# Splitting the first and the last loads of a gated attention and feed-forward kernel

## The chip, the cores and the metric

The kernel runs on one core of one Trainium2 chip. The metric is the device time of one execution in microseconds. Times are medians over repeated executions. The profile is of one further execution. Its span runs from the first to the last recorded instruction, and the execution's own time is a little longer than the span.

## The reference, cut to what matters

Four sequences each decode one token `x` of 512 numbers. One branch is attention with 32 heads over a cache of 4096 keys and values of 128 numbers each, the other a gated feed-forward net. A sigmoid gate mixes the two. All data is float32.

```python
q = (x @ wq).reshape(B, Sq, H, Dh).transpose(0, 2, 1, 3)
scores = einsum("bhqd,bhkd->bhqk", q, k_cache) * (Dh ** -0.5)
o = einsum("bhqk,bhkd->bhqd", softmax(scores), v_cache)
a = o.transpose(0, 2, 1, 3).reshape(B, Sq, H * Dh) @ wo
b = (gelu(x @ w_gate) * (x @ w_up)) @ w_down
g = sigmoid((x * gate_w).sum(-1, keepdims=True))
return g * a + (1 - g) * b
```

`wq` is 512 x 4096, `wo` is 4096 x 512, `w_gate` and `w_up` are 512 x 1792, `w_down` is 1792 x 512. The two caches hold 268 MB each.

## The kernel before, in words

**Tiles.** The caches are cut into 32 steps: four heads of one sequence per step. A step's keys are a tile of 128 partitions by 64 KB (each partition holds 128 whole keys of one head, contiguous in memory), and its values another of the same shape. There are two tiles for keys, `K[0]` and `K[1]`, and one for values, `V`. The weights `wq` have the same shape (128 partitions, four rows of the matrix in each) and are put into `V` before the first values need it.

**Queues.** Every load and store is issued by SyncE, through the helper `load` (L125), whose `dma_start` is L127. The trace therefore puts all DMA issues on L127. SyncE issues in program order and waits between issues until the tile that is to be overwritten is free. Each named load has a semaphore of its own, which counts to 16 when the load has landed.

**The start.** SyncE issues `wq` into `V` (L136), `x` into four partitions (L138), `gate_w` into the same four partitions of another tile (L140), and the first two key tiles. TensorE turns `x` (L163), the gate is worked out from `x` and `gate_w` (L170 to L182, with a matmul at L176), and after that TensorE waits for `have_xT` and `got_q` (L188) and multiplies `x` by `wq` (L193). ScalarE and TensorE turn the result into `QT` (L199 to L211), and the first query is spread over the partitions as `QB[0]` (L218, L221).

**The steps.** `keys(i)` (L266 on) waits for a key tile, multiplies it by the query on VectorE (L269), sums each key's products (L271), and finds the maximum. ScalarE makes the weights (L289). TensorE, in a loop of its own, multiplies them with the values (L231) once these have landed. SyncE issues keys `i + 2` when the sums of step `i` are done (L310) and values `i + 1` when the matmuls of step `i` are done (L313).

**The end.** Into the two key tiles go the weights of the feed-forward net, and then `wo`. `wo` has 32 rows in each partition. Eighteen of them are loaded behind `w_down` in `K[1]`, in two loads of 10 and 8 rows (L326). The last fourteen are loaded into `K[0]` in the sizes of `PIECES` (L55), one load per size (L361 to L364), issued as soon as the feed-forward net no longer needs this tile. A row is 2 KB in each partition, 256 KB in all.

TensorE takes the pieces in order (L418 to L430): it waits for piece `k`, and then runs four matmuls for each of its rows, one per quarter of the 512 outputs (in the trace each is two). VectorE copies the sum out (L432), SyncE stores it (L433).

```python
    PIECES = (4, 4, 3, 2, 1)
    got_q = load(V, wq.rearrange("(p c) n -> p (c n)", c=KC), name="got_q")
    PE.wait(have_xT, got_q)
        PE.wait(got_w[k])
```

Of the kernel before, what the change touches and what calls it, by code (L numbers as in the profile page):

```python
# [34 lines left out]
def tile_gated_mix(ctx: ExitStack, tc: tile.TileContext, x, kc, vc, wq, wo, w_gate, w_up, w_down, gate_w, out):  # L35
    nc = tc.nc
    P = 128
# [3 lines left out]
    KC = DM // P  # L41
# [10 lines left out]
    W1 = (TW - DR * DM) // DM  # L52
    WR = TW // DM
    W0 = 10
    PIECES = (4, 4, 3, 2, 1)  # L55
    BASE = 24576
    scale = 1.0 / math.sqrt(D)
    c_gelu = math.sqrt(2.0 / math.pi)
# [22 lines left out]
    V = kv.tile([P, TW], F32, name="v")  # L81
# [25 lines left out]
    def semaphore(name):  # L107
        counters.append(ctx.enter_context(nc.semaphore(name)))
        return counters[-1]
# [3 lines left out]
    PE = Line(nc.tensor, semaphore("pe"))  # L113
# [11 lines left out]
    def load(dst, src, sem=None, name=None):  # L125
        sem = sem or semaphore(name)
        nc.sync.dma_start(dst, src).then_inc(sem, 16)  # L127
        return sem, 16
# [4 lines left out]
    def load_v(i):  # L133
        load(V, heads(vc, i), sem_v)

    got_q = load(V, wq.rearrange("(p c) n -> p (c n)", c=KC), name="got_q")  # L136
    x_sb = o[:B]
    got_x = load(x_sb, x.rearrange("b s d -> (b s) d"), name="got_x")  # L138
    gw = gs[:B]
# [4 lines left out]
    p0 = PL.do(nc.gpsimd.memset(ident, 0.0))  # L144
# [21 lines left out]
    for c in range(KC):  # L166
        have_xT = DV.do(nc.vector.tensor_copy(xT[:, c], xT_ps[:, c, :, None].to_broadcast([P, B, 8])))  # L167
# [17 lines left out]
    HB = HG // 2  # L185
    PO = [po, bank[6]]
    w = V.rearrange("p (c n) -> p c n", c=KC)
    PE.wait(have_xT, got_q)  # L188
    for c in range(KC):
        for s in range(2):  # L190
            for j in range(4):
# [125 lines left out]
    f, down = K[0], K[1]  # L317
# [42 lines left out]
    r0 = 0  # L360
    for n in PIECES:  # L361
        got_w.append(load(f[:, r0 * DM:(r0 + n) * DM], wo_rows[:, (W1 + r0) * DM:(W1 + r0 + n) * DM],
                          name=f"got_w{r0}"))
# [53 lines left out]
    i = 0  # L417
    for k, n in enumerate(PIECES):  # L418
        if k == 1:
# [40 lines left out]
```

## Time and profile before

| | us |
|---|---|
| median of 3 runs | 1312.04 |
| lowest and highest run | 1311.94, 1312.5 |
| the profiled execution's own time | 1312.45 |
| its span | 1310.7 |
| VectorE busy | 1142.5 |
| TensorE busy with matmuls | 390.0 |
| ScalarE busy | 108.7 |

The page's lines in the prediction read as follows. The row `DMA` gives, in 40 equal slices of the span, the busy share of the 16 DMA engines in tenths. The row `q1` is the queue that SyncE fills: packets, MB, and the share of the 16 engines' span that its packets took. The row of percentages by engine is the chain of work that ended last. A row that begins with `L269` is a group of instructions: line, engine, operation, tile written and read, shapes, count, busy time and mean in ns of one, then the idle time of the engine ahead of them and what ended it. Rows such as `k<-in_A_k_cache SPq` are DMA issues: count, KB each where it is given, and the median time in us from issue to landing.

Rows that begin with a time are from the timeline: start, duration, engine, line, operation, tiles, shape, count, and in brackets the idle time ahead and its releaser. Rows that begin with two times joined by a colon are stretches: length, then busy time and count for TensorE, its weight loads, VectorE, ScalarE and GpSimd, then TensorE's granted clock, the DMA share and GB/s. Where such a row was asked for one line alone, it has TensorE's two columns only. A packet counts with its whole size and duration in the stretch in which it starts.

### The profile page before, as it was taken

To read this page: it belongs to the slowest core of one execution; us is meant where nothing else is said; L and a number is where in the kernel's file an instruction comes from. 1 tells how busy PE (TensorE), PEld (TensorE's weight loads), DVE (VectorE), ACT (ScalarE), POOL (GpSimd) and SP (SyncE) were. 2 spreads that over 40 slices of the span, in tenths; PEclk is the share of its full clock that TensorE was granted. 3 is DMA by queue.
4 is the path that set the end of the run, shared out by engine and by line. 5 is a ranking of instruction groups with operands and counts; after the bars stand their busy time and mean duration, and the time that the engine had idled before them with its cause. 6 is when DMAs were issued, how large, how long until landed. Compare 5 with 4: busy or idle time off the path is not lost.

```text
span 1310.7 us, 6525 instructions
## 1 busy us (share of the span) xinstructions
PE 390.0 (30%) x2766; PEld 136.1 (10%) x2766; DVE 1142.5 (87%) x263; ACT 108.7 (8%) x360; POOL 0.7 (0%) x6
## 2 busy tenths in 40 slices
PE   2132123333213333312333321233231133332147
PEld 0010001111001111000111100011010011100012
DVE  1799999999989899998989989998998999899850
ACT  0000111000000000000000000000000000000010
POOL 0000000000000000000000000000000000000000
PEclk9665566666556666656666655666655666665578
DMA  9999999999999999999999999999999999999998
GB/s 417 416 447 428 436 443 422 444 420 448 426 438 438 426 444 420 448 422 442 436 428 444 420 444 424 440 438 428 446 420 444 422 442 436 428 448 418 434 430 342
DMA packets 10846, 564.80 MB, mean 431 GB/s; under 512 B 1212, under 2 KB 1228, under 8 KB 1620
## 3 DMA queue, kind: packets, MB, share of 16 engines
q1 hardware_dynamic: 10836, 564.69, 99.5%
q8 instruction: 4, 0.07, 0.0%
q14 instruction: 6, 0.05, 0.0%
HBM read 564.67 MB, written 0.01 MB: 431 GB/s over the span
## 4 chain that ended last, share of the span: by engine, by line
DMA 51%; DVE 48%; PE 1%; issue 0%; SPq 0%; ACT 0%
DMA k<-in_A_k_cache 45%; DVE k L269 24%; DVE SC L271 24%; DMA k<-in_B_w_up 3%; DMA k<-in_A_wo 3%; PE bank L338 0%; PE bank L428 0%; SPq L127 0%; DVE m L273 0%; DVE k L354 0%; DVE mt L274 0%; DVE k L351 0%; DVE k L352 0%; DVE nm L275 0%; ACT k L349 0%
## 5 line engine op out<-in xcount | busy, mean ns | idle before, releaser
L269 DVE TENSOR_TENSOR k<-k,QB 128x16384 f32<-128x16384 f32 x32 | 551.2, 17225 | 82.6 <-DMA k<-in_A_k_cache 82.6
L271 DVE TENSOR_REDUCE SC<-k 128x128 f32<-128x16384 f32 x32 | 551.0, 17220 | 1.1
L231 PE MATMUL bank<-v,PM 128*16 128x512 f32 x2048 | 294.7, 740 | 569.8 <-PEq L258 555.7
L231 PEld LDWEIGHTS bank<-v,PM 128*16 128x16 f32 x2048 | 69.4, 113 | 768.5 <-issue 754.3
L224 PE MATMUL bank<-RS,ones 128*128 128x4 f32 x64 | 17.7, 347 | 288.0 <-PEq L256 288.0
L308 ACT ACTIVATE o<-bank 128x512 f32<-128x512 f32 x31 | 18.5, 597 | 869.2 <-PE bank L231 869.2
L289 ACT ACTIVATE PM<-SC,nm 32x128 f32<-32x128 f32 x128 | 66.0, 516 | 200.9 <-DVE nm L275 199.4
L224 PEld LDWEIGHTS bank<-RS,ones 128*128 128x128 f32 x64 | 15.8, 306 | 294.3 <-issue 294.3
L237 PE MATMUL bank<-pick,o 128*128 128x4 f32 x256 | 32.9, 252 | 25.1 <-PEq L260 25.1
L237 PEld LDWEIGHTS bank<-pick,o 128*128 128x128 f32 x256 | 31.0, 191 | 53.6 <-issue 52.7
L280 DVE RECIPROCAL ri<-bank 128x4 f32<-128x4 f32 x32 | 5.5, 173 | 22.5 <-PE bank L237 22.5
L289 ACT ACTIVATION_READ_ACCUMULATOR PM<-SC,nm 32x1 f32 x128 | 25.1, 196 | 0.0
L167 DVE COPY xT<-bank 128x32 f32<-128x32 f32 x4 | 0.5, 182 | 21.5 <-PE bank L163 21.5
L218 PE MATMUL bank<-ident,QX 128*128 128x128 f32 x64 | 15.0, 316 | 1.5 <-ACT QX L215 1.5
L221 ACT ACTIVATE QB<-bank 128x128 f32<-128x128 f32 x32 | 8.9, 278 | 47.3 <-PE bank L218 47.3
L432 DVE COPY res<-bank 128x128 f32<-128x128 f32 x1 | 0.3, 292 | 12.5 <-PE bank L428 12.5
L273 DVE TENSOR_REDUCE m<-SC 128x1 f32<-128x128 f32 x32 | 9.2, 286 | 1.1
L215 ACT ACTIVATE QX<-QT 128x128 f32<-128x128 f32 x32 | 9.9, 308 | 2.4 <-DVE QT L209 1.6
L209 DVE COPY QT<-bank 128x16 f32<-128x16 f32 x8 | 0.9, 180 | 10.5 <-PE bank L205 10.5
L218 PEld LDWEIGHTS bank<-ident,QX 128*128 128x128 f32 x64 | 9.7, 192 | 1.9 <-ACT QX L215 1.1
L193 PE MATMUL bank<-v,xT 128*32 128x512 f32 x64 | 9.5, 760 | 0.0
L338 PE MATMUL bank<-k,xT 128*32 128x448 f32 x64 | 8.1, 659 | 2.6 <-DMA k<-in_B_w_up 2.6
(57 smaller groups left out, 63.5 us busy)
## 6 DMA issues: line engine op xcount, KB each, us to landing
k<-in_B_w_gate SPq DMA_DIRECT2D x1, 3584.0 KB, 31.9
k<-in_B_w_up SPq DMA_DIRECT2D x1, 3584.0 KB, 40.0
k<-in_B_w_down SPq DMA_DIRECT2D x1, 3584.0 KB, 29.5
k<-in_A_wo SPq DMA_DIRECT2D x1, 2560.0 KB, 35.2
k<-in_A_wo SPq DMA_DIRECT2D x1, 2048.0 KB, 39.6
k<-in_A_wo SPq DMA_DIRECT2D x2, 1024.0 KB, 33.5
k<-in_A_wo SPq DMA_DIRECT2D x1, 768.0 KB, 35.9
k<-in_A_k_cache SPq DMA_DIRECT2D x32, 42.7
```

Of the source, the lines that this page charges most:

```text
L193: t = nc.tensor.matmul(PO[s][32 * j:32 * j + 32], xT[:, c, :], w[:, c, n0:n0 + HB * D], start=c == 0, stop=c == KC - 1)
L215: return nc.scalar.activation(QX, QT[:, b, HT * g:HT * g + HT, None].to_broadcast([P, HT, PH]), AF.Copy)
L218: return nc.tensor.matmul(qp[:, :D], QX.rearrange("p h k -> p (h k)"), ident, start=True, stop=True)
L221: return AC.do(nc.scalar.activation(QB[i % 2], qp[:, :D], AF.Copy, scale=scale))
L224: return nc.tensor.matmul(tot, ones, RS, start=True, stop=True)
L231: t = nc.tensor.matmul(po[32 * c:32 * c + M], p[:, j * M:(j + 1) * M], V[:, j * RJ * D:(j + 1) * RJ * D], start=j < 4, stop=j >= n - 4)
L237: t = nc.tensor.matmul(quo, o[:, j * D:(j + 1) * D], pick[:, j, :], start=j == 0, stop=j == RJ - 1)
L269: DV.wait(DV.do(nc.vector.tensor_tensor(k, k, QB[i % 2][:, None, :].to_broadcast([P, R, D]), op=OP.mult)))
L271: summed[i] = DV.do(nc.vector.tensor_reduce(sc, k, axis=AX.X, op=OP.add))
L273: DV.wait(DV.do(nc.vector.tensor_reduce(m1, sc, axis=AX.X, op=OP.max)))
L289: t = nc.scalar.activation(PM[s, :, h], SC[i % 2][s, :], AF.Exp, bias=NM[i % 2][s, :], scale=1.0, accum_out=RS[s, h:h + 1])
L308: nc.scalar.activation(o, po, AF.Copy).then_inc(token_a, 1)
```

## The change

The first load, `wq` into `V`, becomes two: partitions 0 to 15, and then partitions 16 to 127. TensorE waits for both before its first matmul with `wq`. The last fourteen rows of `wo` come in six loads instead of five: the piece of two rows becomes two pieces of one row. What is computed, and in which order, stays the same.

```diff
-    PIECES = (4, 4, 3, 2, 1)
+    PIECES = (4, 4, 3, 1, 1, 1)
...
-    got_q = load(V, wq.rearrange("(p c) n -> p (c n)", c=KC), name="got_q")
+    wq_rows = wq.rearrange("(p c) n -> p (c n)", c=KC)
+    got_q = [load(V[p0:p1], wq_rows[p0:p1], name=f"got_q{p0}") for p0, p1 in ((0, 16), (16, P))]
...
-    PE.wait(have_xT, got_q)
+    PE.wait(have_xT, *got_q)
```

## The prediction

> **What bounds the kernel now.** I read the page's summary first, then the chain of work that ended last, then the queue's own waits, and last the two ends of the span, since the change touches only the first load and the last ones.
>
> ```profile
> span 1310.7 us, 6525 instructions
> DMA  9999999999999999999999999999999999999998
> q1 hardware_dynamic: 10836, 564.69, 99.5%
> DMA 51%; DVE 48%; PE 1%; issue 0%; SPq 0%; ACT 0%
> L269 DVE TENSOR_TENSOR k<-k,QB 128x16384 f32<-128x16384 f32 x32 | 551.2, 17225 | 82.6 <-DMA k<-in_A_k_cache 82.6
> k<-in_A_k_cache SPq DMA_DIRECT2D x32, 42.7
> v<-in_A_v_cache SPq DMA_DIRECT2D x32, 29.3
> v<-in_A_wq SPq DMA_DIRECT2D x1, 22.2
> ```
>
> The loads bound it. One queue carries 564.69 MB and holds the 16 DMA engines busy for 99.5% of the span: 564.69 MB / (16 x 0.995 x 1310.7 us) = 27.1 GB/s for each engine. The chain names VectorE for 48%, but VectorE idles 82.6 us in 32 rounds (2.6 us in each) until a key tile lands. A tile is 128 rows of 65,536 B, eight rows per engine. One row takes 65,536 / 27.1 = 2.42 us, a tile 19.35 us. The keys are issued 42.7 us ahead of their landing and the values 29.3 us, so when a load is issued there are some 23 or 10 us of older work in front of it. Nothing in the middle can make up for a delay of the DMA engines: **time lost in the first load is lost at the end**, and VectorE, 2.6 us ahead in each round, merely waits later.
>
> The two ends:
>
> ```profile
> 0.96 0.39 SPq L127 DMA_DIRECT2D v<-in_A_wq  x1
> 1.41 0.37 SPq L127 DMA_DIRECT2D o<-in_A_x  x1
> 2.12 0.91 SPq L127 DMA_DIRECT2D k<-in_A_k_cache  x2
> 23.42 0.61 PE L163 MATMUL bank<-ident,o 4*128 4x4 f32 x4 [23.42 <-DMA o<-in_A_x]
> 26.60 9.51 PE L193 MATMUL bank<-v,xT 128*32 128x512 f32 x64
> 40.90 0.28 ACT L221 ACTIVATE QB<-bank 128x128 f32<-128x128 f32 x1 [0.62 <-PE bank L218]
> 42.58 17.22 DVE L269 TENSOR_TENSOR k<-k,QB 128x16384 f32<-128x16384 f32 x1 [3.70 <-DMA k<-in_A_k_cache]
> ...
> 1304.57 2.76 PE L428 MATMUL bank<-k,o 128*32 128x128 f32 x48 [0.71 <-DMA k<-in_A_wo]
> 1305.82 1.05 PEld L428 LDWEIGHTS bank<-k,o 128*32 128x32 f32 x24 [0.29 <-DMA k<-in_A_wo]
> 1307.39 0.29 DVE res L432
> ```
>
> The weights of the queries land at 0.96 + 22.2 = 23.16 us, x a little later, and the first keys at 42.55. At the end the last 48 matmuls run almost without a break to 1307.37, then the copy and the store.
>
> **Part 1: the first load as 16 and 112 rows.** The bytes are the same. SP issues one load more (0.39 us by the row at 0.96), which moves x, gate_w and both first key loads by that much. They wait in the queue until 23 us anyway (the keys are issued at 2.12 and used at 42.58), so this costs nothing; without that cover it is 0.4 us. TensorE has one wait more ahead of L193, behind which its whole sequence is queued, but L193 starts at 26.60, 3.4 us after the weights have landed, because the gate's matmul ahead of it waits for x. Cost nothing, and 3.4 us of cover if the second part lands later than the first.
>
> What counts is how fast 16 neighbouring rows can be written. No load of before has that shape, so bounds first. Every large load covers 128 partitions, eight per engine. If each engine keeps its pace, its single row takes 2.42 us: **no loss**. If only the write paths of 16 partitions' share (2 of 16) carry it, 1 MiB takes as long as a whole tile, 19.35 us: a loss of 16.9 us. The nearest row is the load of x: four rows to partitions 0 to 3, 8 KB, right behind the weights. TensorE has it at 23.42, 0.26 us after the weights; about 0.04 us of that is the step from landing to start that the chain shows as issue:
>
> ```profile
> 1304.52 0.04 issue
> ```
>
> At 27.1 GB/s 8,192 B take 0.30 us on one path and 0.08 us on four. The 0.22 us left are nearer to one path for four neighbouring partitions. It is thin, since the row doesn't tell which engines carried x, but it is the only row of this kind. Four partitions to a path put 16 rows on 4 paths, four engines on each: 4 x 2.42 = 9.7 us, **a loss of 7.25 us**, and the engines cannot go on to their next row before.
>
> [...]
>
> Then the 112 rows, seven to an engine if they are shared out evenly and in order. Engine boundaries at sevens no longer fall on groups of four partitions, so engines meet on a path while other paths are idle. Bounds: nothing, if they meet nowhere, and 7 x 2.42 = 16.9 us, if the worst-placed engine shares its path in every row. The slowest engine counts, as the next tile is used when all of it has landed. Of its seven rows I take three as shared with one other engine, each at half pace: 3 x 2.42 = **7.25 us**, a choice a little under the middle.
>
> [...]
>
> A gain belongs to the same part: a shorter first load might start the engines sooner. The stretches of the start:
>
> ```profile
> 1.00:2.00 1.00, 0.00 (x0) 0.00 (x0) 0.90 (x5) 1.00 (x1) 0.45 (x2) 1.00 0.20 66
> 2.00:2.40 0.40, 0.00 (x0) 0.00 (x0) 0.40 (x3) 0.19 (x1) 0.00 (x0) 1.00 5.63 1802
> 2.40:2.90 0.50, 0.00 (x0) 0.00 (x0) 0.12 (x2) 0.00 (x0) 0.00 (x0) 1.00 0.73 262
> 2.90:3.40 0.50, 0.00 (x0) 0.00 (x0) 0.00 (x0) 0.00 (x0) 0.00 (x0) 1.00 0.32 131
> 3.40:5.00 1.60, 0.00 (x0) 0.00 (x0) 0.00 (x0) 0.00 (x0) 0.00 (x0) 1.00 0.09 41
> ```
>
> The last two columns book a packet where it starts: most engines begin between 2.0 and 2.4 us, the last after 3.4. Between nothing and 1.5 us (all engines as early as the first) can be gained. I take 0: the row at 0.96 ends its issue at 1.35, no sooner than x's with its four rows, so a small issue is no quicker.
>
> **Part 2: the last rows as 1, 1, 1 instead of 2, 1.**
>
> ```profile
> 1269.53 0.81 SPq L127 DMA_DIRECT2D k<-in_A_wo  x2
> k<-in_A_wo SPq DMA_DIRECT2D x1, 768.0 KB, 35.9
> k<-in_A_wo SPq DMA_DIRECT2D x1, 512.0 KB, 36.2
> k<-in_A_wo SPq DMA_DIRECT2D x1, 256.0 KB, 36.5
> ```
>
> The two-row piece lands at 1269.53 + 36.2 = 1305.7 to 1305.8, the last row some 0.6 us later, at 1306.4. The sequencer stood 0.29 us (PEld at 1305.82) until the two rows were there. With single rows the first lands 0.6 us sooner, that wait goes, and what is late next is the last row itself: landing 1306.4, a start 0.04 later, and 8 matmuls. 24 matmuls a microsecond is the pace there:
>
> ```profile
> 1306.00:1307.00 1.00, 1.00 (x24) 0.80 (x19) 0.50 0.06 18
> L428 PE MATMUL bank<-k,o x112: 268/273/422, 1300.4 to 1306.9; 128*32 128x128 f32 x112
> ```
>
> So 8 take 0.33 us, the last of them up to 0.42 by itself (the second row's longest): 1307.2 instead of 1307.37. Gain 0.1 to 0.2, at most 0.29; I take **0.1**. One more load is issued 0.43 us behind its neighbour, 36 us before it lands: nothing. Its overhead in the engines is unknown, between 0 and the 0.4 us that two issues lie apart; the pieces of 3, 2 and 1 rows land in proportion to their rows, so I take 0.
>
> **The sum.** The profiled execution took 1312.45 us (span 1310.7, 1.75 around it); 1312.45 + 7.25 + 7.25 - 0.1 = 1326.85. The median of the runs is 0.41 lower, so the forecast is **1326.4 us**. One discount stays open: the engines do not end together.
>
> ```profile
> 1304.00:1305.00 1.00, 0.43 (x12) 0.44 (x16) 0.86 0.35 141
> 1305.00:1306.00 1.00, 1.00 (x24) 0.71 (x20) 0.50 0.20 76
> ```
>
> From 1304 on 0.35, then 0.20 of them are busy, so a few end up to 2 us after the rest. If those that lose most at the start are not these, up to 2 us of the loss vanish.
>
> **The rivals.**
>
> *Only the first load is slow.* The 112 rows flow as before. For it: seven rows in a row leave each engine time to shift past its neighbour. Against it: while engines queue for a path, another path idles. 1312.04 + 7.25 - 0.1 = 1319.2, between 1316.5 and 1322.5.
>
> *The engines keep their pace, so it is not slower.* Place: the write of the first 16 rows. It decides if a write path serves each engine, not a group of partitions; then only part 2 and the start count: 1312.04 - 0.1 = 1311.9, between 1310.5 (1.5 us gained at the start) and 1313. For it: the 27.1 GB/s per engine is the same in all loads, whichever partitions an engine writes. Against it: x.
>
> *The 112 rows meet all the time.* If engine e takes every sixteenth row, all 16 engines write 16 neighbouring partitions in each step, each at a quarter of its pace: another 7 x 7.25 = 50.8 us, 1370 us. Against it: the profile shows no load shared out like that.
>
> *The change doesn't do what it says*: the early start of the first load buys nothing since L193 waits for both parts and, before that, for x. That is so in each case above and is in the sum.
>
> **How the numbers follow.** Forecast (1322.5 to 1330): 0.42. Only the first load: 0.24. Pace kept: 0.22. Above 1330: 0.11. Gain over 0.2% by a start that brings more than the 1.5 us: 0.01. The range leaves out the last two and the fringe of others: 1311.0 to 1330.0; the forecast's own is 1322.5 to 1330. About 0.2% (2.6 us) is what a measurement of this kernel can tell from no change. Faster 0.01, same 0.22, slower 0.77.
>
> **What would show it.** Right: the weights land some 14 us later than 23.16 from the first issue, the stretch from 3 to 12 us moves about a quarter of 431 GB/s, the first key product starts near 57 instead of 42.58, every later round is shifted by the same amount, and VectorE's idle time per round stays 2.6 us. If the stretch from 3 to 12 us moves 430 GB/s, the step on the narrow load is wrong. If the key product starts near 50, the step on the 112 rows is. At the end the 0.29 us wait ahead of the last 24 weight loads should be gone. The forecast falls if x was late for a reason of its own, since that row alone chose the value between the bounds.

## The result and the profile after

The changed kernel takes 1333.55 us (median of 6 runs, 1331.57 to 1333.75), the kernel before 1312.03 (6 runs). The ratio is 1.0162, with a 95% interval of 1.0151 to 1.0173: **21.5 us slower**. The forecast was 1326.4 with a range up to 1330.0. The direction was right, and so was the first of the two terms. The second one, for the 112 rows, was half of what it is, because its picture of how engines slow each other was wrong, and the range was too narrow.

The page of the changed kernel first. Lines below L136 of the kernel before have moved down by one.

```profile
span 1331.7 us, 6528 instructions
GB/s 217 378 419 420 441 435 428 439 431 441 429 433 431 439 439 427 437 429 441 431 431 439 431 439 433 431 431 437 439 429 437 429 437 437 429 439 427 429 434 340
q1 hardware_dynamic: 10996, 564.69, 99.5%
L270 DVE TENSOR_TENSOR k<-k,QB 128x16384 f32<-128x16384 f32 x32 | 551.2, 17225 | 84.6 <-DMA k<-in_A_k_cache 84.6
k<-in_A_k_cache SPq DMA_DIRECT2D x32, 42.7
v<-in_A_v_cache SPq DMA_DIRECT2D x32, 29.3
```

The queue moves the same 564.69 MB and is again busy for 99.5% of the span. That share counts the time that packets take, and rows of 64 KB that took 2.4 to 3.6 us in the first load of before now take up to 9.4, so it does not show the loss. The GB/s by slice do: 217 in the first of 40 slices and 378 in the second, where it was 417 and 416, then the old level. The keys and values still land 42.7 and 29.3 us after their issue, as before.

The timeline of the start of the changed kernel:

```profile
0.96 0.87 SPq L127 DMA_DIRECT2D v<-in_A_wq  x2
42.53 0.61 PE L164 MATMUL bank<-ident,o 4*128 4x4 f32 x4 [42.53 <-DMA o<-in_A_x]
45.71 9.82 PE L194 MATMUL bank<-v,xT 128*32 128x512 f32 x64
60.31 0.28 ACT L222 ACTIVATE QB<-bank 128x128 f32<-128x128 f32 x1 [0.62 <-PE bank L219]
63.64 17.22 DVE L270 TENSOR_TENSOR k<-k,QB 128x16384 f32<-128x16384 f32 x1 [5.34 <-DMA k<-in_A_k_cache]
```

The first key product starts at 63.64 instead of 42.58, 21.06 us later, and TensorE's turn of `x` at 42.53 instead of 23.42. Nothing of the 21 us is made up or added in the middle: VectorE's idle time in the 31 rounds after the first is (84.6 - 5.34) / 31 = 2.56 us each, and before it was (82.6 - 3.70) / 31 = 2.55. So the whole loss arises in the first 63 us.

Stretches of the start, of the changed kernel and then of the kernel before; the last two columns are the DMA share and GB/s:

```profile
2.00:12.00 10.00, 0.00 (x0) 0.00 (x0) 0.52 (x3) 0.19 (x1) 0.00 (x0) 1.00 1.33 203
12.00:22.00 10.00, 0.00 (x0) 0.00 (x0) 0.00 (x0) 0.00 (x0) 0.00 (x0) 1.00 0.80 210
22.00:32.00 10.00, 0.00 (x0) 0.00 (x0) 0.00 (x0) 0.00 (x0) 0.00 (x0) 1.00 1.05 262
32.00:42.00 10.00, 0.00 (x0) 0.00 (x0) 0.00 (x0) 0.00 (x0) 0.00 (x0) 1.00 0.97 251
```

```profile
2.00:12.00 10.00, 0.00 (x0) 0.00 (x0) 0.52 (x3) 0.19 (x1) 0.00 (x0) 1.00 1.02 413
12.00:22.00 10.00, 0.00 (x0) 0.00 (x0) 0.00 (x0) 0.00 (x0) 0.00 (x0) 1.00 0.97 419
22.00:32.00 10.00, 6.52 (x34) 2.35 (x38) 2.41 (x10) 0.17 (x1) 0.00 (x0) 1.00 1.08 467
32.00:42.00 10.00, 6.15 (x52) 2.41 (x44) 0.86 (x8) 2.34 (x7) 0.00 (x0) 0.99 1.07 465
```

Both parts of the new first load are slow, and the second one for longer: from 12 to 42 us, while the 112 rows move, the rate is 210 to 262 GB/s where it was 419 to 467. In the trace's packets (64 KB each, one per row) the 16 rows take 7.8 to 9.4 us each instead of 2.4 to 3.6 for the first rows of before. The 112 rows take 4.6 us each in the median. Of an engine's seven rows, the first two take 4.7 to 5.7 us, the third mostly 3.1, the fourth mostly 3.7, and the last three 4.2 to 4.8. **About half pace in five of the seven rows, on every engine,** is what the forecast did not have: it gave three rows of seven to it, and only on the engines that are placed worst.

### The profile page after: what moved, and what is told of

It is laid out like the page before. It is cut to its first block, busy times and chain, and to the rows that moved or that the text cites. A ratio compares the mean times of both kernels' runs of the same rounds, so it can differ in the third digit from the quotient of the medians.

```text
span 1331.7 us, 6528 instructions
## 1 busy us (share of the span) xinstructions
PE 386.2 (29%) x2766; PEld 134.8 (10%) x2766; DVE 1142.4 (86%) x263; ACT 108.7 (8%) x360; POOL 0.7 (0%) x6
## 3 DMA queue, kind: packets, MB, share of 16 engines
q1 hardware_dynamic: 10996, 564.69, 99.5%
## 4 chain that ended last, share of the span: by engine, by line
DMA 50%; DVE 47%; PE 1%; another core or an unknown queue 0%; issue 0%; SPq 0%; ACT 0%; DVEq 0%
DMA k<-in_A_k_cache 41%; DVE k L270 23%; DVE SC L272 23%; DMA o<-in_A_x 3%; DMA k<-in_B_w_up 3%; DMA k<-in_A_wo 3%; PE bank L194 1%; PE bank L339 0%; SPq L127 0%; DVE m L274 0%; ACT v L200 0%; DVE k L355 0%; DVE mt L275 0%; DVE QT L210 0%
## 5 line engine op out<-in xcount | busy, mean ns | idle before, releaser
L270 DVE TENSOR_TENSOR k<-k,QB 128x16384 f32<-128x16384 f32 x32 | 551.2, 17225 | 84.6 <-DMA k<-in_A_k_cache 84.6
L272 DVE TENSOR_REDUCE SC<-k 128x128 f32<-128x16384 f32 x32 | 551.0, 17220 | 1.1
L232 PE MATMUL bank<-v,PM 128*16 128x512 f32 x2048 | 291.7, 734 | 569.8 <-PEq L259 555.4
L281 DVE RECIPROCAL ri<-bank 128x4 f32<-128x4 f32 x32 | 5.5, 172 | 21.8 <-PE bank L238 21.8
```

Source lines behind the costliest of these rows:

```text
L232: t = nc.tensor.matmul(po[32 * c:32 * c + M], p[:, j * M:(j + 1) * M], V[:, j * RJ * D:(j + 1) * RJ * D], start=j < 4, stop=j >= n - 4)
L270: DV.wait(DV.do(nc.vector.tensor_tensor(k, k, QB[i % 2][:, None, :].to_broadcast([P, R, D]), op=OP.mult)))
L272: summed[i] = DV.do(nc.vector.tensor_reduce(sc, k, axis=AX.X, op=OP.add))
```

## The experiments

The experiments are compared with runs of the kernel before on the same chip (1311.99 to 1312.01 us). Four others are ladders, kernels with a series of extra loads ahead of everything; each of these ran once and is read from its trace alone.

### One part at a time

The change without the pieces of `wo`, and the pieces alone:

```diff
+    got_q = [load(V[p0:p1], wq_rows[p0:p1], name=f"got_q{p0}") for p0, p1 in ((0, 16), (16, P))]
```

> Only the first load is split into 16 and 112 rows; the pieces of wo stay 4, 4, 3, 2, 1. Theory (write paths): all of the loss comes from the first load, so 1333.5 us, within 0.5 of the change. Rival (the smaller last pieces, or one more load near the end, cost something): clearly below that, 1333.5 less what they cost. Each would put the landing of the second part at the same time as in the change, 41 to 44 us.

```diff
-    PIECES = (4, 4, 3, 2, 1)
+    PIECES = (4, 4, 3, 1, 1, 1)
```

> Only the last rows of wo come as 4, 4, 3, 1, 1, 1; the first load stays whole. By the step of the prediction on part 2: 1311.9 us, 0.1 faster (0 to 0.3), with the 0.29 us wait ahead of the last 24 weight loads gone. Rival (each more load costs the engines its own overhead at the end): 0 to 0.4 us slower than before.

The split alone takes 1333.82 us (ratio 1.0163, 1.0147 to 1.0178), as much as the change. The pieces alone take 1311.92 us against 1311.99 (ratio 1.0000, 0.9991 to 1.0009): no difference that can be measured. **All of the loss comes from the first load.**

What became of the 0.1 us is seen at the end of the timeline with the pieces alone, and then of a kernel with the old pieces (the split by columns, below). The last row of each is from the stretches; its third number from the end is the granted clock, full in both, and half in the profile of before.

```profile
1304.34 1.10 PE L428 MATMUL bank<-k,o 128*32 128x128 f32 x32 [0.77 <-DMA k<-in_A_wo]
1305.64 0.42 PE L428 MATMUL bank<-k,o 128*32 128x128 f32 x8 [0.20 <-DMA k<-in_A_wo]
1306.26 0.42 PE L428 MATMUL bank<-k,o 128*32 128x128 f32 x8 [0.20 <-DMA k<-in_A_wo]
1306.76 0.29 DVE L432 COPY res<-bank 128x128 f32<-128x128 f32 x1 [12.66 <-PE bank L428]
...
1306.00:1307.00 1.00, 0.49 (x12) 0.16 (x8) 0.24 (x1) 0.00 (x0) 0.00 (x0) 1.00 0.00 0
```

```profile
1305.47 1.05 PE L429 MATMUL bank<-k,o 128*32 128x128 f32 x24 [0.40 <-DMA k<-in_A_wo]
1306.59 0.29 DVE L433 COPY res<-bank 128x128 f32<-128x128 f32 x1 [13.27 <-PE bank L429]
...
1306.00:1307.00 1.00, 0.52 (x14) 0.16 (x8) 0.29 (x1) 0.00 (x0) 0.00 (x0) 1.00 0.05 16
```

With single rows, TensorE waits 0.20 us for each of the last two and runs eight matmuls in 0.42. In both kernels the copy starts 0.53 to 0.54 us after the last landing of the trace (1306.22 and 1306.06): the last row decides, and how the rows ahead of it are cut does not. In the profile of before it was 0.98 us (1306.41 to 1307.39), at half the clock. There, TensorE had not caught up with the two-row piece when the last row came. So a gain would be left only where the clock is low at the end; no run with single rows had it low there, so this is not shown.

### Other cuts of the first load

Halves; then two loads of all 128 partitions, cut by columns; then three loads with the middle first:

```diff
+... for p0, p1 in ((0, 64), (64, P))]
```

> The first load comes as 64 and 64 rows, the pieces of wo as before. Theory (paths of four neighbouring partitions, each path also serving the partitions 32 further, so that 64 neighbours reach half of the paths): each half takes a whole load's 19.35 us, in all 19.35 more, 1331.4 us. Rival (only a narrow first part and shares of seven rows that straddle the groups of four are slow; four rows per engine fit): 0 to 1 us more, 1312 to 1313. Rival (pace in proportion to the partitions covered at a time): also 19.35 more, so this run does not tell that one from the theory; the isolated loads do.

```diff
+    got_q = [load(V[:, n0:n1], wq_rows[:, n0:n1], name=f"got_q{n0}") for n0, n1 in ((0, 2048), (2048, TW))]
```

> The first load comes in two, but both of 128 partitions: the first 8 KB of each row and then the other 56 KB. Pieces of wo as before. Theory (only the paths that a load reaches matter): 1312.0 us, within 0.5 of before. Rival (a split first load costs by itself, by one more load at the head of the queue): several us slower.

```diff
+... for p0, p1 in ((32, 96), (0, 32), (96, P))]
```

> The first load comes in three: partitions 32 to 95, then 0 to 31, then 96 to 127; pieces of wo as before. Theory (paths of four neighbours, shared with the group 32 further): the 64 middle rows reach all 16 paths and take 9.7 us, the two loads of 32 reach eight paths each and take 9.85 us each by the isolated load of 32 (12.29 less 2.44); 29.4 instead of 19.35, so 1322.0 us, faster than the change and the halves although it is one load more. Rival (the pace goes by the number of neighbouring partitions): 64 rows take 19.35 us or more as in the halves, in all at least 39, 1332 us or more.

| first load | us | ratio (95%) |
|---|---|---|
| 64 and 64 rows | 1333.36 | 1.0177 (1.0160 to 1.0194) |
| 8 KB and 56 KB of all rows | 1311.93 | 0.9998 (0.9988 to 1.0007) |
| rows 32 to 95, 0 to 31, 96 to 127 | 1322.61 | 1.0077 (1.0060 to 1.0094) |

A split as such cost nothing here: along the columns it took 1311.93 us against 1312.01 before. Halves cost as much as 16 and 112 rows, 2 us more than was expected of them (one of their four runs took 1338.6 us, which raises the ratio and hardly the median). The three loads, with the same bytes, are 10.9 us faster than the two of the change and 0.6 from the expected 1322.0; timed by themselves, as below, the middle 64 rows took 12.62 us from issue to issue, and rows 0 to 63 took 22.89.

### Single loads, timed by themselves

The ladders have extra loads of `wq` rows into the second key tile, each issued after the landing of the one before:

```diff
+    for n, first, step in PROBES:
+        got = load(K[1][first:first + (n - 1) * step + 1:step], wq_rows[:n], name=f"probe{n}_{first}_{step}")
+        SP.wait(got)
```

> Eleven extra loads of 64 KB rows of wq into the second key tile stand ahead of the first load, each issued when the one before has landed, so that the distance of two issues is the time of one load with some 2 us of fixed time. Number of rows, first partition and step: 128 at 0; 4 at 0; 16 at 0; 16 at 0 by 8; 16 at 0 by 7; 16 at 16 by 7; 32, 64, 96 and 112 at 0; 112 at 16. One row at an engine's pace is 2.42 us. If engines keep their pace: 19.4, 2.4, 2.4, 2.4, 2.4, 2.4, 4.8, 9.7, 14.5, 16.9, 16.9 plus the fixed time. Theory (paths of four neighbours, shared with the partitions 32 further, consecutive rows per engine): 19.4, 9.7, 9.7, 4.8, 4.8, 4.8, 9.7, 19.4 and, for the last three, between 17 and 34 by how often two engines meet. Rival (pace in proportion to the partitions covered): 19.4 for each load of neighbouring partitions, and for 16 rows that are spread out 2.4. Rival (a load whose rows are no power of two per engine is slow for a reason of its own): 96 and 112 slow, but 16 by 7 at 2.4.

Seven of the eleven issues in the timeline of SyncE's queue, from the first ladder (its `dma_start` is L129); the start of one less the start of the one before is the time of the load before:

```profile
0.97 22.13 SPq L129 DMA_DIRECT2D k<-in_A_wq  x2
...
33.74 0.32 SPq L129 DMA_DIRECT2D k<-in_A_wq  x1
45.34 0.63 SPq L129 DMA_DIRECT2D k<-in_A_wq  x1
52.99 0.53 SPq L129 DMA_DIRECT2D k<-in_A_wq  x1
...
134.44 0.31 SPq L129 DMA_DIRECT2D k<-in_A_wq  x1
166.88 0.31 SPq L129 DMA_DIRECT2D k<-in_A_wq  x1
```

The 16 neighbouring rows took 45.34 - 33.74 = 11.60 us, the same 16 rows by steps of eight partitions 7.65. In all, from issue to issue: 128 rows 21.79 (19.35 at pace and 2.44 fixed); 4 at 0 10.98; 16 at 0 11.60; 16 by 8 7.65; 16 by 7 at 0 and at 16 both 7.18; 32 12.29; 64 22.89; 96 31.91; 112 at 0 32.43; 112 at 16 33.97.

This rules out engines that keep their pace, and pace by the number of partitions: 4 rows take as long as 16, and 32 hardly longer, not 19.4. The loads of 16 all read the same 16 rows of `wq` and differ only in where they write, so the reading does not make the difference. The expectations put a model to the test: four neighbouring partitions are written through one path, shared with the group 32 further. No trace shows a path; what can be compared are times. The model gives 9.7 us for 4 and for 16 (measured 8.54 and 9.16 without the fixed time), 4.8 by 8 (5.2), 9.7 for 32 (9.85), 19.4 for 64 at 0 (20.45), and in the next ladder 9.7 for 64 at 32 (10.18). The 8.54 us for four rows, against 2.42 for a row at pace, agree with what the forecast took from the load of `x`, one path for four neighbouring partitions. They do not make that row a proof: in the trace of before, the eight packets of 2 KB that carry `x` and `gate_w` took 0.08 us each, the forecast's own value for four paths, and all had ended at 22.50, before the last row of the weights at 22.79. Why TensorE had `x` only at 23.42 is open. A row of the 64 took 20.45 / 4 = 5.1 us rather than the 4.84 of half pace, which is the 2 us by which the halves were missed.

But one thing did not fit: in both loads by steps of seven, all 16 packets of the trace took 3.9 to 4.8 us, though by the model only four of the engines share a path. The next ladder was to tell why:

> Eleven isolated extra loads ahead of the first load, as in the earlier run of this kind, each issued when the one before has landed; in that run 128 rows took 21.79 us from issue to issue, 19.35 at an engine's pace and 2.44 of fixed time. Rows, first partition, step: 128 at 0; 16 at 32 by 4; 16 at 11 by 7; 16 at 19 by 7; 16 at 0 by 4; 8 at 0 by 4; 8 at 64 by 4; 8 at 3 by 3; 64 at 32; 64 at 16; 64 at 0 by 2. Common to all theories: groups of four neighbouring partitions, a path for each with the group 32 further. By it the loads reach 16, 16, 16, 15, 8, 8, 8, 7, 16, 12 and 8 paths. Theory M (only engines that meet on a path are slowed): 21.8, 4.9, 4.9, 7.3 with 14 of 16 packets at pace, 7.3, 4.9, 4.9, 7.3 with six of eight packets at pace, 12.1, 21.8, 21.8. Theory C (where two engines meet, all the engines of the load are held to their pace): the same times, but in the fourth and eighth load all packets are slow alike. Theory O (an engine is at half pace on any path but the one that it has in a load of 128 rows): 21.8, 4.9, then 7.3 for the third, 7.3, 7.3, 4.9, 7.3 for the seventh, 7.3, 12.1, 21.8, 21.8. Rival (pace by the number of partitions spanned): 64 at 32 as slow as 64 at 0, 22.9.

Measured, in the same order: 128 rows 21.87; 16 at 32 by 4 5.18; 16 at 11 by 7 5.37; 16 at 19 by 7 6.86, with two of 16 packets at 4.1 and 4.3 us and the others under 3.4; 16 at 0 by 4 7.49; 8 at 0 by 4 5.15; 8 at 64 by 4 5.10; 8 at 3 by 3 7.28, with two of eight packets slow; 64 at 32 12.62; 64 at 16 22.59, with all 64 packets slow; 64 at 0 by 2 12.47. Of the loads by steps of four, partitions 0 to 28 took 5.15 us, 0 to 60 took 7.49 and 32 to 92 took 5.18, as the model has it. Theory O falls by the seventh (8 at 64 by 4, 5.10 and not 7.3). Theory C falls in the form in which it was put: a single pair holds up nobody else. Theory M falls by the tenth, if consecutive rows go to an engine: half of the engines then share with none by the model, and their rows are as slow as the rest. The last, 64 rows by steps of two, was expected at 21.8 with consecutive rows and took 12.47, so for it the model with consecutive rows does not hold. How rows are shared out where the count is a power of two was not settled further. The times of the 112 rows fit consecutive ones, as the wide loads below show.

So where the model has one pair of engines on a path, two packets were slow (4.1 and 4.3 us of 16 at 19 by 7), and where it has two, all 16 (3.9 to 4.8 us). The same 16 rows, moved on by one partition at a time, put that to the test:

> Twenty-four isolated extra loads: 128 rows at 0, and then 16 rows by steps of seven partitions from first partition 0, 1, and so on to 22. Each engine has one row, and with paths of four neighbours shared with the group 32 further the loads have no two engines on one path (first partition 11), one such pair (3, 4, 7, 15, 18, 19) or two pairs (all others). An earlier run had all 16 packets slow in two loads with two pairs and only two packets slow in one with one pair. Theory C (two pairs or more hold up all engines, one pair only itself): 5.2 us from issue to issue for 11; about 6.9 with two slow packets for the six with one pair; about 7.2 with all 16 packets at 3.9 us or more for the sixteen with two pairs. Theory M (only the engines that meet are slow): two slow packets with one pair, four with two, the other twelve at 2.4 to 3.3 us. Rival (the place in the row of loads or the time made the two earlier ones slow): slow packets in no relation to the pairs.

**All 23 came out as theory C had them**, but for its bound of 3.9 us, which was a little high. The pairs are those of the model. First partition 11, no pair: 5.09 us, all packets at 2.4 to 3.2. First partitions 3, 4, 7, 15, 18 and 19, one pair: 6.9 to 7.3 us, exactly two packets over 3.9, the others up to 3.4. The sixteen with two pairs: 7.1 to 7.4 us, no packet under 3.5, and all but two of the 256 over 3.8. Stretches of two pairs, one pair and none, one load in each:

```profile
22.90:30.10 7.20, 0.00 (x0) 0.00 (x0) 0.00 (x0) 0.00 (x0) 0.00 (x0) 1.00 0.59 146
44.60:51.50 6.90, 0.00 (x0) 0.00 (x0) 0.00 (x0) 0.00 (x0) 0.00 (x0) 1.00 0.46 152
102.10:107.20 5.10, 0.00 (x0) 0.00 (x0) 0.00 (x0) 0.00 (x0) 0.00 (x0) 1.00 0.54 206
```

The share by the length is the mean packet, as each engine has one: 0.59 x 7.2 = 4.2 us, 0.46 x 6.9 = 3.2, 0.54 x 5.1 = 2.8.

Then the wide loads:

> Twelve isolated extra loads: 128 rows at 0; 48 at 32; 80 at 32; 96 at 16; 96 at 32; 112 at 0, 4, 8, 12 and 16; 32 at 0 by 4; 32 at 48. Consecutive rows are taken for each engine: 3, 5, 6 and 7. Theory C (every row in which two or more pairs of engines meet takes all of them 5.1 us, one with one pair 3.7 on the whole, else 2.42, plus 2.44 fixed): 17.8 for 48, 28.0 for 80, 33.2 for both of 96, 35.4 for each of 112 (35.6 for first partition 8). Theory M (only those that meet are slow, each engine goes on by itself; worked row by row with equal shares): 12.1, 24.2, 26.6, 26.6, and 24.2 for each of 112. An earlier run had 31.9 for 96 at 0, 32.4 for 112 at 0 and 34.0 for 112 at 16. If rows are dealt out otherwise (one row of each sixteen to an engine): 4 paths at a time, 31.4 for 48 and 70 for 112. For 32 at 0 by 4, 7.3 if the engine has the path of its rows to itself, 12.3 with consecutive rows; for 32 at 48, 12.3 by either.

Measured: 48 rows 17.32; 80 26.91; 96 at 16 31.80, at 32 31.97; 112 at 0, 4, 8, 12, 16: 33.84, 32.31, 33.97, 33.33, 33.24. Theory C had 17.8, 28.0, 33.2 twice and 35.4 to 35.6, so it is 3 to 10% too high; theory M, which is the forecast's own picture, had 12.1, 24.2, 26.6 and 24.2. The three rows of 48 decide clearest: 9.7 us and the fixed time by theory M, and they took 14.9 and the fixed time, three rows at half pace. Dealing out by sixteens (70 for 112) falls. 32 rows at 0 by 4 took 8.19, nearer to the 7.3 expected of rows that are not dealt out consecutively, and 32 at 48 took 12.33.

The packets show it row by row. An engine's next packet starts where its last one ends, so the packets of the loads of 48, 80, 96 and 112 rows in the first and the last ladder can be sorted into 75 rows, each written by all 16 engines. The pairs of each row are counted by the model, with consecutive rows for each engine. The 62 rows with two or more pairs took 4.15 to 5.13 us on the mean, the twelve with one pair 3.3 to 4.1, and the only one without (the fourth of 112 at 8) 3.04: no row is out of order. So the rival of the first ladder, that a load is slow because its count per engine is no power of two, falls: within one such load the row without a pair is the fast one, at 3.04 us. Why the rows with one pair or none took more than 2.42 us is not shown.

### The two terms in place

One extra load at the head of the queue, with all else as before:

```diff
+    got_extra = load(K[1][0:16], wq_rows[:16], name="got_extra")
...
+    SP.wait(got_extra)
     load_k(1)
```

> The kernel before with one extra load at the head of the queue, 16 rows of 64 KB to the neighbouring partitions 0 to 15 of the second key tile (whose own load waits for it, behind 39 us of other loads); the first load stays whole. It measures the first term of the sum in place. Theory (four paths for 16 rows): 9.2 us more by the isolated load (11.60 less 2.44), 1321.2 us; of that 2.4 are the bytes themselves and 6.8 the narrowness. Rival (a narrow load costs nothing by its shape when others follow it in the queue): 2.4 more, 1314.4.

With `K[1][32:93:4]` instead:

> The same extra load of 16 rows, but to partitions 32 to 92 by steps of four, which reach all 16 paths. Theory: 2.4 to 2.7 us more than before, 1314.5 us. Rival (a load of 16 rows is slow as such, wherever they go): as slow as the neighbouring 16, 1321 us.

With `K[1][16:P]` and 112 rows:

> The same with an extra load of 112 rows to partitions 16 to 127, the shape of the second part of the change. At the engines' pace it takes 16.9 us, 1328.9 us. By the prediction's second term (three of seven rows shared) 24.2 us, 1336.2. Theory after the isolated loads (as soon as two pairs of engines meet, all are held up): 31.5 us by the isolated load (33.97 less 2.44), 1343.5, of which 14.6 are lost to the shape. Rival (the 112 rows are only slow behind the 16 neighbouring ones): 1329.

| extra load | us | ratio (95%) |
|---|---|---|
| 16 rows, partitions 0 to 15 | 1321.11 | 1.0067 (1.0050 to 1.0084) |
| 16 rows, partitions 32 to 92 by 4 | 1314.89 | 1.0023 (1.0014 to 1.0033) |
| 112 rows, partitions 16 to 127 | 1341.81 | 1.0224 (1.0207 to 1.0241) |

The first key products of the three (L272 in these kernels), in this order:

```profile
51.84 17.23 DVE L272 TENSOR_TENSOR k<-k,QB 128x16384 f32<-128x16384 f32 x1 [4.77 <-DMA k<-in_A_k_cache]
```

```profile
45.19 17.22 DVE L272 TENSOR_TENSOR k<-k,QB 128x16384 f32<-128x16384 f32 x1 [4.52 <-DMA k<-in_A_k_cache]
```

```profile
74.00 17.23 DVE L272 TENSOR_TENSOR k<-k,QB 128x16384 f32<-128x16384 f32 x1 [5.15 <-DMA k<-in_A_k_cache]
```

Against 42.58 the first is 9.26 us later, 6.84 more than its 2.42 us of bytes; the second 2.61; the third 31.42, 14.5 more than its 16.9 us of bytes. 6.84 + 14.5 = 21.3, and the change delays the same row by 21.06. The terms add up at the start. At the end the third kernel is 29.8 us later and not 31.4, so that by the medians the two terms are 6.7 and 12.9 us, 19.6 together, 2 us less than the change costs. That would fit the discount that the prediction left open (engines that lost most at the start need not be those that end last), but no run isolates it.

## Why the prediction was wrong

**What bounds the kernel, and that a delay at the head of the queue stays.** Right: 21.06 us at the first key product, 21.5 at the end, 2.56 us of idle time per round against 2.55 before.

**The narrow load, 7.25 us.** Right: 6.84 in place, and from 3 to 12 us the changed kernel moved 117 GB/s, about the quarter of 431 that was named as a sign. The value came from the load of `x` on four neighbouring partitions, and the load of 4 rows timed by itself fits it: 8.54 us without the fixed time, for one row per engine, where a row at pace takes 2.42. But the packets of `x` took 0.08 us each and don't show it, so choosing the right value from that row was in part luck. By itself the load of 16 rows moved 1.049 MB / 11.60 us = 90 GB/s with the fixed time and 1.049 / 9.16 = 114 without, near the 117 in place.

**The 112 rows, 7.25 us. This step failed**: "Of its seven rows I take three as shared with one other engine, each at half pace". It is 14.5 us, twice that, at the first key product (12.9 at the end, as the term stands alone), and near the upper bound of 16.9 that the same step gave. The picture behind it was that an engine is slow only in the rows that it shares itself. Worked through with the model of the paths (theory M of the last ladder), that picture gives 24.2 - 2.44 - 16.9 = 4.9 us, so the three rows were more than it bears, and still too few; the first key product came at 63.64 and not near 57. In the wide loads the rows with two or more pairs by the model took 4.15 to 5.13 us on the mean, about half pace, and by the same count five of the seven rows of the 112 have two pairs, and the third and fourth have one. In the changed kernel's packets the third and fourth are the rows in which 14 of 16 took about 3.1 and 3.7 us, and two 4.4 to 4.9. Five rows at about half pace and two in between: that is the upper bound, less what the two rows save.

**The range** ended at 1330.0, although this bound was in the text: 1312.04 + 7.25 + 16.9 - 0.1 = 1336.1 was not ruled out by any row. The only rival priced above 1330 was another mechanism (rows dealt out by sixteens, 1370 us), which the 112 timed alone (33 us, not 70) rule out.

**The covers.** Right: the later issues cost nothing (the split by columns, with one issue more, is at 1311.93), and TensorE's second wait neither.

**The early start.** Right at 0, as far as can be measured: with 8 KB of all rows first, the first load is short and goes to all 128 partitions, and the time is 1311.93 against 1312.01.

**The pieces, 0.1 us.** Within what can be measured, nothing. The wait of 0.29 us was read at a granted clock of 0.50; in the two runs shown at 1.00 the last row's landing decided both ways.

**The rivals.** Only the first load slow (1319.2) and the pace kept (1311.9) are out.

## What to carry to other kernels

Ask of each load which partitions its rows reach at a time, and not only how many bytes and engines it has: from issue to issue, 16 rows took 11.60 us at partitions 0 to 15 and 5.18 at 32 to 92 by steps of four. Cut across the partitions, the first load of 128 rows cost 21.5 us, and cut along the rows it cost nothing (1311.93 us against 1312.01); with a DMA queue that is busy for 99.5% of the span, none of the 21.5 us came back. Where a bound is given for an effect whose rule is unknown, keep it in the range. The DMA share of 99.5% was the same in both kernels and did not say whether the engines moved their packets at pace; GB/s by stretch told, with 203 against 413 from 2 to 12 us.

## What the runs showed of the hardware

- In loads of 16 rows by steps of seven the packets of 64 KB took 2.4 to 3.2 us where the model of the paths has no two DMA engines on one path. With one pair two of the 16 took 4.0 to 5.1 us and the others up to 3.4, and with two pairs all 16 took 3.6 to 5.3. Why is open.
- 64 neighbouring rows need not be slow: from issue to issue, partitions 32 to 95 took 12.62 us, 0 to 63 22.89 and 16 to 79 22.59.
- Loads of 48, 80, 96 and 112 rows took 4.3 to 5.0 us for each row of an engine, wherever the rows began, e.g. 14.9 us for the three of 48 without the fixed time; a row with two or more pairs by the model took 4.15 to 5.13 us on the mean, the one without a pair 3.04.
